# Top-32 attention and a quick-GELU MLP on one core: slots of two interleaved score tiles, packed array halves and MLP units of 128 tokens

## The chip, the cores and the metric

The kernel runs on one core of a Trainium2 chip. Its engines work side by side, each through its own list of instructions: TensorE (PE in the profile, with its loads of the stationary operand as PEld), VectorE (DVE), ScalarE (ACT), GpSimd (POOL), and SyncE (SP), which here issues DMAs. The metric is the device time of one execution in microseconds; lower is better. The kernel before takes 2505.77 us, the median of three runs from 2504.82 to 2506.19 us.

## The reference

```python
scores = scale * np.matmul(q, k.transpose(0, 1, 3, 2))        # q, k, v: (8, 8, 576, 64), scale 1/8
kth = np.partition(scores, -top_k, axis=-1)[..., -top_k:-top_k + 1]   # top_k = 32
scores = np.where(scores >= kth, scores, -1000000000.0)
attn = np.exp(scores - np.max(scores, axis=-1, keepdims=True))
attn = attn / (np.sum(attn, axis=-1, keepdims=True) + 1e-09)
x = np.matmul(attn, v).transpose(0, 2, 1, 3).reshape(4608, 512)
h = x @ w_in                                                   # (512, 2048)
return (h * (1.0 / (1.0 + np.exp(-1.702 * h))) @ w_out).astype(np.float32)   # (2048, 512)
```

All of it is in float32. The two weights come as float64, and the kernel rounds their bits to float32 itself.

## The kernel before

The 64 heads go in 32 pairs. `transpose_pair` turns q and k of a pair so that the first head's 64 dimensions lie on partitions 0 to 63 and the second's on 64 to 127. A head has 576 queries: four tiles of 128 rows, and a ninth tile of the pair that holds the last 64 rows of both. `scores` (from L167) multiplies a tile (`sc`, L181) into PSUM: 512 and 64 columns, contracted over the 64 partitions of its head. There the scores stay. VectorE finds the 32nd largest of each row in four rounds: the eight largest (MAX8, L185 and L196), then their removal (MATCH_VALUE_LOAD and MATCH_REPLACE8, L193), three times. Meanwhile GpSimd makes the negated maximum (`low`, L187), ScalarE the exponentials of all 576 scores (`e`, L189), and at the end VectorE multiplies these by the comparison with the 32nd largest (`pr`, L198).

`transpose_probs` (L208, L211) turns `pr` on TensorE, five transposes to a tile, and ScalarE copies them to SBUF as `pt`. `values` (L224) takes `pt` as the stationary operand and v, with a column of ones beside it for the denominators, as the moving one of 65 columns; VectorE takes reciprocals (L232, L234) and ScalarE divides (L236). `transpose_out` (L259, L262) turns the outputs of a pair once more into `xT`.

The MLP runs in twelve units of 384 tokens. `hidden` (L285) makes 128 hidden units of 384 tokens from four products; ScalarE takes tanh (L294) and VectorE the gate (L295). `project` (L304) multiplies with `wout` into 512 columns. The 32 pieces of weights, one to each of the first 32 tiles, are rounded by four VectorE instructions (L124, L127, L130, L131), one on ScalarE (L132) and four on GpSimd (L133 to L136).

The order of the program is a loop over tiles (from L342): each step issues the scores and the top-k of one tile, then what `at` put down for it from earlier tiles, then as many pieces of the MLP as a credit in columns allows. The framework's own scheduler then orders each engine's list. Every float32 product is two TensorE instructions in the trace, each with its load of the stationary operand; a transpose is one.

## Time and profile before

| | before |
|---|---|
| median of three runs | 2505.77 us (2504.82 to 2506.19) |
| span of the profiled execution | 2504.9 us |
| TensorE busy | 2276.3 us (91%) |
| VectorE busy | 1949.9 us (78%) |
| ScalarE busy | 686.9 us (27%) |
| GpSimd busy | 265.5 us (11%) |
| mean granted clock of TensorE | 0.881 of full speed |

The profiled execution has no time beside its span; the span stands 0.9 us under the median of the runs. Busy is the time in which an engine has at least one instruction in work; TensorE's instructions are pipelined, so lengths of single ones add up to more than that, and the start of the next instruction tells more than the end of one. The granted clock is TensorE's: 1.00 is 2.4 GHz and 0.50 is 1.2 GHz, its two levels. A rate is read from starts in the rows in order of time.

### The profile page before, as it was taken

The page shows a single profiled execution, that of the slowest core. Times are in us where ns is not written, and L with a number is a line of the kernel's source. Part 1 is how long each engine was busy: PE and PEld are TensorE (multiplying, and loading weights), DVE is VectorE, ACT ScalarE, POOL GpSimd, SP SyncE. Part 2 cuts the span into 40 slices and gives each one's busy share as a digit, 9 for nine tenths or more (in the row PEclk, how much of TensorE's full clock was granted, in tenths as well). Part 3 has the DMA queues.
Part 4 walks back from the last instruction along what each step waited for, and adds up shares of the span by engine and source line. Part 5 has one row for each costly group of instructions (what it writes and reads, how often), then busy time and mean ns, then how long its engine had stood idle before and what let it go on. Part 6 is the DMA issues. An engine that isn't in the chain of part 4 may idle for free.

```text
span 2504.9 us, 25884 instructions
## 1 busy us (share of the span) xinstructions
PE 2276.3 (91%) x9088; PEld 1399.2 (56%) x9088; DVE 1949.9 (78%) x3680; ACT 686.9 (27%) x1637; POOL 265.5 (11%) x490
## 2 busy tenths in 40 slices
PE   5556879998999999999999999999999999999999
PEld 3344556655655565665555565565555555665554
DVE  6999878887888888888888887888888887798200
ACT  2222223222222332232222332232322332232200
POOL 5777100000000000000000000000000000000000
PEclk9755559995789899999899999999899998999999
DMA  3222000000000000000000000000000000000000
GB/s 105 82 77 72 15 14 11 19 23 15 5 15 23 19 15 19 19 15 23 10 15 23 19 15 18 19 15 23 19 5 23 19 15 24 4 6 9 4 13 13
DMA packets 122818, 56.21 MB, mean 22 GB/s; under 512 B 116288, under 2 KB 116288, under 8 KB 122688
## 3 DMA queue, kind: packets, MB, share of 16 engines
q1 hardware_dynamic: 119808, 45.11, 7.1%
q0 software_dynamic: 2880, 9.44, 1.0%
q8 instruction: 73, 1.20, 0.2%
q14 instruction: 57, 0.47, 0.1%
HBM read 45.09 MB, written 9.44 MB: 22 GB/s over the span
## 4 chain that ended last, share of the span: by engine, by line
PE 72%; DVE 12%; issue 9%; POOL 4%; ACT 2%; SPq 0%; DMA 0%; POOLq 0%; ACTq 0%
PE ph L285 19%; PE po L304 17%; PE o L224 15%; PE sc L181 13%; PE tp L208 5%; DVE left L193 4%; DVE top L196 3%; ACT e L189 1%; PE tp L163 1%; DVE top L185 1%; PE tp L211 1%; POOL room L135 1%; POOL room L134 1%; POOL room L133 1%; DVE pr L198 1%
## 5 line engine op out<-in xcount | busy, mean ns | idle before, releaser
L196 DVE MAX8 top<-left 128x8 f32<-128x576 f32 x864 | 656.2, 759 | 22.3
L285 PE MATMUL ph<-xT,win 128*128 128x384 f32 x1536 | 563.5, 515 | 4.2 <-ACT xp L236 4.2
L304 PE MATMUL po<-wout,gT 128*128 128x512 f32 x1152 | 543.1, 614 | 2.1 <-ACT ob L313 2.1
L224 PE MATMUL o<-v_l,pt 128*128 128x65 f32 (+3 forms) x3200 | 499.4, 305 | 2.6 <-ACT pt L209 2.6
L224 PEld LDWEIGHTS o<-v_l,pt 128*128 128x128 f32 (+3 forms) x3200 | 440.1, 208 | 70.7 <-issue 11.5
L181 PE MATMUL sc<-k_t,q_t 64*128 64x512 f32 (+3 forms) x1280 | 450.4, 510 | 0.4 <-ACT k_t L164 0.4
L193 DVE MATCH_REPLACE8 left<-top,left 128x576 f32<-128x576 f32 x576 | 427.4, 742 | 0.0
L208 PE MATMUL tp<-ident,pr 128*128 128x128 f32 x1152 | 207.4, 310 | 209.4 <-DVE pr L198 205.1
L285 PEld LDWEIGHTS ph<-xT,win 128*128 128x128 f32 x1536 | 290.7, 198 | 189.1 <-issue 20.8
L189 ACT ACTIVATE e<-sc,low 128x576 f32<-128x576 f32 x288 | 213.2, 740 | 551.5 <-POOL low L187 551.4
L181 PEld LDWEIGHTS sc<-k_t,q_t 64*128 64x128 f32 (+1 forms) x1280 | 216.6, 204 | 238.7 <-issue 237.7
L304 PEld LDWEIGHTS po<-wout,gT 128*128 128x128 f32 x1152 | 210.4, 193 | 224.4 <-issue 207.8
L208 PEld LDWEIGHTS tp<-ident,pr 128*128 128x128 f32 x1152 | 158.3, 160 | 311.7 <-issue 289.5
L209 ACT COPY pt<-tp 128x512 f32<-128x512 f32 x288 | 168.6, 585 | 332.9 <-PE tp L208 332.5
L295 DVE SCALAR_TENSOR_TENSOR gT<-th,ph 128x384 f32<-128x384 f32 x192 | 105.8, 551 | 191.2 <-ACT th L294 190.5
L187 POOL TENSOR_SCALAR low<-top 128x1 f32<-128x1 f32 x288 | 64.6, 224 | 1699.1 <-DVE top L185 1665.9
L198 DVE SCALAR_TENSOR_TENSOR pr<-sc,top,e 128x576 f32<-128x576 f32 x288 | 230.4, 800 | 0.0
L185 DVE MAX8 top<-sc 128x8 f32<-128x576 f32 x288 | 215.4, 748 | 10.3 <-PE sc L181 10.1
L193 DVE MATCH_REPLACE8 left<-top,sc 128x576 f32<-128x576 f32 x288 | 215.4, 748 | 0.0
L294 ACT ACTIVATE th<-ph 128x384 f32<-128x384 f32 x192 | 94.3, 491 | 379.8 <-PE ph L285 379.8
L236 ACT ACTIVATE xp<-o,rden 128x64 f32<-128x64 f32 (+1 forms) x320 | 75.6, 313 | 230.3 <-DVE rden L234 230.3
L193 DVE MATCH_VALUE_LOAD left<-top,sc 128x8 f32 x288 | 26.5, 92 | 128.8 <-ACT e L189 125.2
(48 smaller groups left out, 865.5 us busy)
## 6 DMA issues: line engine op xcount, KB each, us to landing
out_dram<-ob POOLq DMA_DIRECT2D x36, 256.0 KB, 2.3
q_l<-in_q_dram SPq DMA_DIRECT2D x64, 128.0 KB, 2.4
k_l<-in_k_dram SPq DMA_DIRECT2D x64, 128.0 KB, 2.5
v_l<-in_v_dram SPq DMA_DIRECT2D x64, 128.0 KB, 2.4
room<-in_moe_w_in_dram SPq DMA_DIRECT2D x16, 512.0 KB, 3.8
room<-in_moe_w_out_dram SPq DMA_DIRECT2D x16, 512.0 KB, 3.4
q_l<-in_q_dram SPq DMA_DIRECT2D x32, 32.0 KB, 2.3
k_l<-in_k_dram SPq DMA_DIRECT2D x32, 32.0 KB, 2.4
```

Source lines behind the costliest of these rows:

```text
L181: nc.tensor.matmul(sc[rows, c], lhsT=d["qT"][on, cols], rhs=d["kT"][on, c])
L185: nc.vector.max(top[:], sc)
L189: nc.scalar.activation(e[:], sc, AF.Exp, bias=low[:])
L193: nc.vector.match_replace(nxt[:], top[:], left, LOWEST)
L196: nc.vector.max(top[:], left)
L198: nc.vector.scalar_tensor_tensor(out=pr[:], in0=sc, scalar=top[:, 7:8], in1=e[:], op0=ALU.is_ge, op1=ALU.mult)
L208: nc.tensor.transpose(full[:, c * P : (c + 1) * P], pr[:, c * P : (c + 1) * P], ident[:])
L209: nc.scalar.copy(out=pt[:, 0:NF, :].rearrange("p c r -> p (c r)"), in_=full[:, 0:FULL])
L224: nc.tensor.matmul(o[0:rows, g, :], lhsT=d["pt", s][0:keys, c, cols], rhs=d["v"][0:keys, c, j, :], start=(c == 0), stop=(c == NS - 1),)
L285: nc.tensor.matmul(ph[:, 0:UNIT], lhsT=win[:, c, f * P : (f + 1) * P], rhs=xts[m][:, c, u * UNIT : (u + 1) * UNIT], start=(c == 0), stop=( ...
L295: nc.vector.scalar_tensor_tensor(out=mlp["gT"][:, f, :], in0=th[:], scalar=1.0, in1=ph[:, 0:UNIT], op0=ALU.add, op1=ALU.mult)
L304: nc.tensor.matmul(po[:], lhsT=mlp["gT"][:, f, r * P : (r + 1) * P], rhs=wout[:, f, :], start=(f == 0), stop=(f == FC - 1),)
```

## The change

- A slot takes two score tiles: the same 128 queries of both heads of a pair, or the last 64 queries of two pairs. There are 18 slots to a batch, 144 in all. Their score products alternate between the heads, whose operands lie on opposite 64 partitions, and go to two PSUM tiles in pieces of 288 columns. ScalarE copies both to SBUF.
- VectorE's top-k alternates between the two tiles, instruction by instruction. Its last step no longer multiplies: it writes the negated score, and one less that for scores that are left out. Scores are 1/256 of their size, so that the exponential, taken afterwards with a scale of -256, is 0 for these. ScalarE sums the denominators in the same instruction, and GpSimd divides the probabilities.
- The last 64 columns of the two tiles lie side by side and are turned together (nine transposes for two tiles). For the value product v is now the stationary operand, 64 columns wide, and the turned probabilities move; the two heads write opposite halves of the output's partitions. The outputs come out as `xT`, so no transposes follow.
- The MLP's units are 128 tokens. One slot has a quarter of a unit: 16 hidden products of 128 columns, one tanh, one gate of 512 columns, four projections.
- In the first eleven slots three pieces of weights each are rounded, with temporaries in two buffers; one GpSimd step of before becomes ScalarE's absolute value, and the last is VectorE's.
- The order is written by hand: the framework's scheduler is off, and `slot(n)` fixes what each engine does. Outputs are stored from SyncE's queue.

```diff
-    UNIT = 384
+DOWN = 256.0
+    G = 4
+    FIRST = (TAIL, 0)
+    MAIN = (0, FULL + 2 * TAIL)
...
+    raws = pool("raws", 5)
+    temps = pool("temps", 2)
+    scp = pool("scp", 3)
+    prp = pool("prp", 2)
+    ps_s = pool("ps_s", 2, space=PSUM)
+    ps_t = pool("ps_t", 2, space=PSUM)
+    ps_h = pool("ps_h", 1, space=PSUM)
+    ps_p = pool("ps_p", 1, space=PSUM)
...
+        power = temps.tile([P, PIECE], F32, name="power")
+        part = temps.tile([P, PIECE], F32, name="part")
+        size = temps.tile([P, PIECE], F32, name="size")
+        nc.scalar.mul(out=part[:], in_=low, mul=2.0**-52)
+        nc.scalar.activation(size[:], high.bitcast(F32), AF.Abs)
...
+        def powers():
+            nc.vector.tensor_single_scalar(power[:].bitcast(U32), bits, 0xFF800000, op=ALU.bitwise_and)
+            nc.gpsimd.tensor_tensor(out=part[:], in0=part[:], in1=power[:], op=ALU.mult)
+            nc.gpsimd.tensor_tensor(out=part[:], in0=part[:], in1=dst, op=ALU.add)
+        def normal():
+            nc.vector.scalar_tensor_tensor(
+                out=dst, in0=size[:], scalar=LEAST_HIGH, in1=part[:], op0=ALU.is_ge, op1=ALU.mult
+            )
+        return [cut, sign, powers], normal
...
+    slots = []
+    for b in range(B):
+        slots += [(b, t, (hp, hp)) for t in range(NF) for hp in range(NP)]
+        slots += [(b, NF, (hp, hp + 1)) for hp in range(0, NP, 2)]
+    N = len(slots)
...
+    def scores(n):
+        b, t, hps = slots[n]
+        ps = [ps_s.tile([P, 2, 512], F32, name="s_ps") for _ in range(2)]
+        if t < NF:
+            parts = [(j, j, slice(0, P), slice(t * P, (t + 1) * P)) for j in range(2)]
+        else:
+            parts = [(i, j, slice(j * TAIL, (j + 1) * TAIL), slice(FULL, S)) for i in range(2) for j in range(2)]
+        for c in range(2):
+            for i, j, rows, cols in parts:
+                on = slice(j * D, (j + 1) * D)
+                nc.tensor.matmul(
+                    ps[i][rows, c, 0:HALF],
+                    lhsT=qT[b, hps[i]][on, cols],
+                    rhs=kT[b, hps[i]][on, FIRST[i] + c * HALF : FIRST[i] + (c + 1) * HALF],
+                )
+        sc = st[n]["sc"] = scp.tile([P, 2, S], F32, name="sc")
+        for i in range(2):
+            nc.scalar.copy(out=sc[:, i, :].rearrange("p (c k) -> p c k", c=2), in_=ps[i][:, :, 0:HALF])
+    def topk(n):
+        sc = st[n]["sc"]
+        top = st[n]["top"] = small.tile([P, 2, TOPK], F32, name="top")
+        left = lefts.tile([P, 2, S], F32, name="left")
+        def largest(r, i):
+            nc.vector.max(top[:, i, 8 * r : 8 * r + 8], (left if r else sc)[:, i, :])
+        def remove(r, i):
+            nc.vector.match_replace(
+                left[:, i, :], top[:, i, 8 * r : 8 * r + 8], (left if r else sc)[:, i, :], LOWEST
+            )
+        def leave_out(i):
+            nc.vector.scalar_tensor_tensor(
+                out=sc[:, i, :],
+                in0=sc[:, i, :],
+                scalar=top[:, i, TOPK - 1 : TOPK],
+                in1=sc[:, i, :],
+                op0=ALU.is_lt,
+                op1=ALU.subtract,
+            )
+        ops = []
+        for r in range(TOPK // 8):
+            ops += [lambda r=r, i=i: largest(r, i) for i in range(2)]
+            if r < TOPK // 8 - 1:
+                ops += [lambda r=r, i=i: remove(r, i) for i in range(2)]
+        return ops + [lambda i=i: leave_out(i) for i in range(2)]
+    def lowest(n):
+        low = st[n]["low"] = small.tile([P, 2], F32, name="low")
+        nc.gpsimd.tensor_scalar(low[:], st[n]["top"][:, :, 0], -DOWN, None, op0=ALU.mult)
+    def exponentials(n):
+        sc, low = st[n]["sc"], st[n]["low"]
+        pr = st[n]["pr"] = prp.tile([P, 2 * S], F32, name="pr")
+        den = st[n]["den"] = small.tile([P, 2], F32, name="den")
+        for i in range(2):
+            nc.scalar.activation(
+                pr[:, i * S : (i + 1) * S], sc[:, i, :], AF.Exp, bias=low[:, i : i + 1], scale=-DOWN,
+                accum_out=den[:, i : i + 1],
+            )
+    def divide(n):
+        den, pr = st[n]["den"], st[n]["pr"]
+        some = small.tile([P, 2], F32, name="some")
+        nc.vector.tensor_scalar_add(some[:], den[:], 1e-9)
+        rden = small.tile([P, 2], F32, name="rden")
+        nc.vector.reciprocal(rden[:], some[:])
+        for i in range(2):
+            on = pr[:, i * S : (i + 1) * S]
+            nc.gpsimd.tensor_scalar(on, on, rden[:, i : i + 1], None, op0=ALU.mult)
+    def turn(n):
+        pr = st[n]["pr"]
+        pt = st[n]["pt"] = ptp.tile([P, 2 * NF + 1, P], F32, name="pt")
+        for i in range(2):
+            tp = ps_t.tile([P, 512], F32, name="tp")
+            for c in range(NF):
+                nc.tensor.transpose(tp[:, c * P : (c + 1) * P], pr[:, MAIN[i] + c * P : MAIN[i] + (c + 1) * P], ident[:])
+            nc.scalar.copy(out=pt[:, i * NF : (i + 1) * NF, :].rearrange("p c r -> p (c r)"), in_=tp[:])
...
+    def values(n):
+        b, t, hps = slots[n]
+        pt = st[n]["pt"]
+        outs = []
+        if t < NF:
+            groups = [(0, [(j, slice(0, P), j) for j in range(2)])]
+        else:
+            groups = [(i, [(i, slice(j * TAIL, (j + 1) * TAIL), i) for j in range(2)]) for i in range(2)]
+        for i, heads in groups:
+            main, tail = vv[b, hps[i]]
+            o = ps_t.tile([P, 512], F32, name="o", tag="tp")
+            for c in range(NF + 1):
+                for j, (tile_, cols, half) in enumerate(heads):
+                    dst = o[j * D : (j + 1) * D, 0 : cols.stop - cols.start]
+                    if c < NF:
+                        lhsT, rhs = main[:, c, j, :], pt[:, tile_ * NF + c, cols]
+                    else:
+                        on = slice(half * TAIL, (half + 1) * TAIL)
+                        lhsT, rhs = tail[on, j, :], pt[on, 2 * NF, cols]
+                    nc.tensor.matmul(dst, lhsT=lhsT, rhs=rhs, start=(c == 0), stop=(c == NF))
+            outs.append((o, hps[i]))
...
+    def hidden():
+        if not ready:
+            return
+        xT, rows = ready[0]
+        g = hidden_at["g"]
+        ph = ps_h.tile([P, G, P], F32, name="ph")
+        for i in range(G):
+            f = g * G + i
+            for c in range(CC):
+                nc.tensor.matmul(
+                    ph[:, i, :],
+                    lhsT=win[:, c, f * P : (f + 1) * P],
+                    rhs=xT[:, c, :],
+                    start=(c == 0),
+                    stop=(c == CC - 1),
+                )
...
+            th = thp.tile([P, G, P], F32, name="th")
+            nc.scalar.activation(th[:], ph[:], AF.Tanh, scale=0.851)
+            to_gate.append((ph, g, rows, th))
+    def gate():
+        if to_gate:
+            ph, g, rows, th = to_gate.pop()
+            gT = gtp.tile([P, G, P], F32, name="gT")
+            nc.vector.scalar_tensor_tensor(
+                out=gT[:], in0=th[:], scalar=1.0, in1=ph[:], op0=ALU.add, op1=ALU.mult
+            )
+            to_project.append((gT, g, rows))
...
+    RATE = 3
+    by_slot = [list(range(i, min(i + RATE, NPIECE))) for i in range(0, NPIECE, RATE)]
+    for n, some in enumerate(by_slot):
+        for x in some:
+            at(n - 1, load_piece, x)
+    def slot(n):
+        todo = later.pop(n, [])
+        for fn, args in todo:
+            if fn is not prepare:
+                fn(*args)
+        if 0 <= n - 2 < N:
+            turn(n - 2)
+        if n >= NPIECE // RATE - NG + 1:
+            hidden()
+        if 0 <= n - 1 < N:
+            exponentials(n - 1)
+        if 0 <= n - 2 < N:
+            turn_tail(n - 2)
+        tanh()
+        rounding = [round_piece(x) for x in by_slot[n]] if 0 <= n < len(by_slot) else []
+        project()
+        for fn, args in todo:
+            if fn is prepare:
+                fn(*args)
+        if n + 1 < N:
+            scores(n + 1)
+        if 0 <= n - 2 < N:
+            values(n - 2)
+        chain = topk(n) if 0 <= n < N else [lambda: None] * 16
+        first = [op for ops, _ in rounding for op in ops]
+        last = [op for _, op in rounding]
+        for i, op in enumerate(chain):
+            op()
+            if i == 1 and 0 <= n < N:
+                lowest(n)
+            if i == 5 and 0 <= n - 1 < N:
+                divide(n - 1)
+            if i == 9:
+                gate()
+            if i and first:
+                first.pop(0)()
+            elif last and i > 11:
+                last.pop(0)()
+        for op in first + last:
+            op()
+    with tc.manual_schedule():
+        for n in range(-1, N + 2):
+            slot(n)
+        n = N + 2
+        while ready or to_project:
+            slot(n)
+            n += 1
```

`turn` makes eight transposes of `pr`, `turn_tail` the ninth; `load`, `load_v` and `prepare` are what `load_pair` and `transpose_pair` were, at fixed slots.

VectorE's list at a tile and a half in the middle of the kernel before, where `left` is the row with maxima removed, `top` the eight largest, and `gT` the gate:

```order
L185 MAX top<-sc 128x8
L198 SCALAR_TENSOR_TENSOR pr<-sc,top,e 128x576
L295 SCALAR_TENSOR_TENSOR gT<-th,ph 128x384
L193 MATCH_REPLACE left<-top,sc 128x576
L196 MAX top<-left 128x8
L193 MATCH_REPLACE left<-top,left 128x576
L232 TENSOR_SCALAR den<-o 128x4
L196 MAX top<-left 128x8
L234 RECIPROCAL rden<-den 128x4
L193 MATCH_REPLACE left<-top,left 128x576
L196 MAX top<-left 128x8
```

A whole slot on VectorE in the changed kernel:

```order
L239 MAX top<-sc 128x8 x2
L242 MATCH_REPLACE left<-top,sc 128x576 x2
L239 MAX top<-left 128x8 x2
L280 TENSOR_SCALAR some<-den 128x2
L282 RECIPROCAL rden<-some 128x2
L242 MATCH_REPLACE left<-top,left 128x576 x2
L239 MAX top<-left 128x8 x2
L382 SCALAR_TENSOR_TENSOR gT<-th,ph 128x512
L242 MATCH_REPLACE left<-top,left 128x576 x2
L239 MAX top<-left 128x8 x2
L247 SCALAR_TENSOR_TENSOR sc<-sc,top 128x576 x2
```

Before, each maximum and removal needs the one just ahead of it. Now two equal instructions follow each other, one for each tile, and what an instruction needs stands two places ahead.

TensorE's list for two tiles of before, where `sc` are scores, `tp` transposes, `o` values, `ph` hidden units and `po` projections:

```order
L208 MATMUL tp<-ident,pr 128x128 x4
L211 MATMUL tp<-ident,pr 64x128
L285 MATMUL ph<-xT,win 128x384 x2
L181 MATMUL sc<-k_t,q_t 128x512
L181 MATMUL sc<-k_t,q_t 128x64
L285 MATMUL ph<-xT,win 128x384 x6
L208 MATMUL tp<-ident,pr 128x128 x4
L211 MATMUL tp<-ident,pr 64x128
L181 MATMUL sc<-k_t,q_t 128x512
L181 MATMUL sc<-k_t,q_t 128x64
L285 MATMUL ph<-xT,win 128x384 x2
L224 MATMUL o<-v_l,pt 128x65 x15
```

A slot on TensorE in the changed kernel (`s_ps` are its scores, `v_l` and `v_t` the values' main part and last 64 rows):

```order
L293 MATMUL tp<-ident,pr 128x128 x8
L358 MATMUL ph<-xT,win 128x128 x16
L299 MATMUL tp<-ident,pr 128x128
L396 MATMUL po<-wout,gT 128x512 x4
L223 MATMUL s_ps<-k_t,q_t 128x288 x4
L323 MATMUL o<-pt,v_l 64x128 x8
L323 MATMUL o<-pt,v_t 64x128 x2
```

The hidden products have a third of the columns, and the value products write 64 partitions each; the scores are the next slot's, the turned probabilities and values those of two slots ago.

ScalarE's list in the weights' stage of before (`room` holds a piece's scaled low words) for two tiles:

```order
L189 ACTIVATE e<-sc,low 128x576
L209 COPY pt<-tp 128x512
L212 COPY pt<-tp 64x128
L132 ACTIVATE room<-room 128x512
L189 ACTIVATE e<-sc,low 128x576
L132 ACTIVATE room<-room 128x512
L209 COPY pt<-tp 128x512
L212 COPY pt<-tp 64x128
```

And one slot of the changed kernel in that stage (`part` are the scaled low words, `size` the absolute values):

```order
L294 COPY pt<-tp 128x512 x2
L272 ACTIVATE pr,den<-sc,low 128x576 x2
L300 COPY pt<-tp 128x128
L132 ACTIVATE part<-raw 128x512
L133 ACTIVATE size<-raw 128x512
L132 ACTIVATE part<-raw 128x512
L133 ACTIVATE size<-raw 128x512
L132 ACTIVATE part<-raw 128x512
L133 ACTIVATE size<-raw 128x512
L230 COPY sc<-s_ps 128x576 x2
L329 COPY xT<-o 128x128
```

The score copies for the next slot now stand behind the scaling of three pieces.

## Rows read from the trace of the kernel before

**Rows 1.** The page's head: span, TensorE's busy time, the chain that ended last.

```profile
span 2504.9 us, 25884 instructions
...
PE 2276.3 (91%) x9088; PEld 1399.2 (56%) x9088; DVE 1949.9 (78%) x3680; ACT 686.9 (27%) x1637; POOL 265.5 (11%) x490
...
PE 72%; DVE 12%; issue 9%; POOL 4%; ACT 2%; SPq 0%; DMA 0%; POOLq 0%; ACTq 0%
```

**Rows 2.** Line 185's instructions: duration min/median/max in ns, first and last start.

```profile
L185 DVE MAX8 top<-sc x288: 739/748/767, 10.1 to 2317.2; 128x8 f32<-128x576 f32 x144
```

**Rows 3.** TensorE in order of time: start, length in us, instructions [idle before <-releaser].

```profile
1197.69 3.70 PE L304 MATMUL po<-wout,gT 128*128 128x512 f32 x8
1201.23 0.60 PE L208 MATMUL tp<-ident,pr 128*128 128x128 f32 x4
...
1201.87 1.29 PE L181 MATMUL sc<-k_t,q_t 64*128 64x512 f32 x4
1203.09 1.47 PE L224 MATMUL o<-v_l,pt 128*128 128x65 f32 x10
1208.60 1.08 PE L208 MATMUL tp<-ident,pr 128*128 128x128 f32 x4 [4.04 <-DVE pr L198]
```

**Rows 4.** Stretches: us, busy PE, PEld, DVE, ACT, POOL, granted clock, DMA share, GB/s.

```profile
1208.70:1219.40 10.70, 10.70 (x37) 6.76 (x38) 9.32 (x19) 1.60 (x4) 0.29 (x2) 0.50 0.12 28
...
1062.60:1072.70 10.10, 10.10 (x27) 6.68 (x28) 4.59 (x11) 1.67 (x6) 0.15 (x1) 0.50 0.00 0
1072.80:1205.80 133.00, 131.07 (x571) 78.26 (x570) 113.33 (x218) 40.40 (x96) 5.59 (x22) 1.00 0.08 20
```

**Rows 5.** TensorE in order of time, ahead of the second of these stretches.

```profile
1058.77 4.42 PE L224 MATMUL o<-v_l,pt 128*128 128x65 f32 x30
```

**Rows 6.** VectorE in order of time, through parts of two tiles.

```profile
1604.72 0.76 DVE L196 MAX8 top<-left 128x8 f32<-128x576 f32 x1
1605.40 0.75 DVE L185 MAX8 top<-sc 128x8 f32<-128x576 f32 x1
1606.07 0.80 DVE L198 SCALAR_TENSOR_TENSOR pr<-sc,top,e 128x576 f32<-128x576 f32 x1
...
1607.33 0.75 DVE L193 MATCH_REPLACE8 left<-top,sc 128x576 f32<-128x576 f32 x1
1607.99 0.55 DVE L295 SCALAR_TENSOR_TENSOR gT<-th,ph 128x384 f32<-128x384 f32 x1
1608.45 0.75 DVE L196 MAX8 top<-left 128x8 f32<-128x576 f32 x1
1609.24 0.09 DVE L193 MATCH_VALUE_LOAD left<-top,left 128x8 f32 x1
1609.32 0.74 DVE L193 MATCH_REPLACE8 left<-top,left 128x576 f32<-128x576 f32 x1
```

**Rows 7.** TensorE's value products from one start, in two windows of different end.

```profile
1234.65 0.50 PE L224 MATMUL o<-v_l,pt 128*128 128x65 f32 x3
...
1234.65 0.72 PE L224 MATMUL o<-v_l,pt 128*128 128x65 f32 x5
```

**Rows 8.** TensorE in order of time: the ninth score tile of a pair.

```profile
1266.34 1.20 PE L181 MATMUL sc<-k_t,q_t 64*64 64x512 f32 x8
```

**Rows 9.** The page's groups: count, busy us, mean ns, idle time before.

```profile
L189 ACT ACTIVATE e<-sc,low 128x576 f32<-128x576 f32 x288 | 213.2, 740 | 551.5 <-POOL low L187 551.4
```

**Rows 10.** The same for the rounding of weights, shapes kept apart.

```profile
L133 POOL TENSOR_SCALAR room<-room 128x512 f32<-128x512 f32 x32 | 52.2, 1631 | 0.9 <-DVE room L131 0.9
...
L134 POOL TENSOR_TENSOR room<-room 128x512 f32<-128x512 f32 x32 | 40.6, 1268 | 54.7 <-DVE room L130 46.5 <-ACT room L132 6.4 <-ACT e L189 1.8
...
L127 DVE SCALAR_TENSOR_TENSOR wout<-room,wout 128x512 uint32<-128x512 uint32 x16 | 15.2, 953 | 0.0
...
L124 DVE TENSOR_SCALAR wout<-room 128x512 uint32<-128x512 uint32 x16 | 10.6, 664 | 0.0
```

**Rows 11.** ScalarE at the end of the span: the last output copy.

```profile
2499.47 0.60 ACT L313 ACTIVATE ob<-po 128x512 f32<-128x512 f32 x1 [13.19 <-PE po L304]
```

More of the change, by code (lines that the diff above doesn't have):

```diff
@@ new lines, with load @@
+    qT, kT, vv = {}, {}, {}
+    loaded = {}
+    def load(name, b, hp):
+        src = q if name == "q" else k
+        t = loaded[name, b, hp] = loads.tile([P, NF + 1, 2, D], F32, name=f"{name}_l")
+        for j in range(2):
+            nc.sync.dma_start(
+                t[:, 0:NF, j, :], src[b, 2 * hp + j, 0:FULL, :].rearrange("(t p) d -> p t d", p=P)
+            )
+        nc.sync.dma_start(
+            t[0:TAIL, NF, :, :], src[b, 2 * hp : 2 * hp + 2, FULL:S, :].rearrange("h p d -> p h d")
+        )
@@ L243, in head_values @@
-    def head_values(p, j):
-        values(p, [(j * NF + t, slice(0, P), j, t) for t in range(NF)], P)
-    def tail_values(p):
-        values(p, [(2 * NF, slice(j * TAIL, (j + 1) * TAIL), j, NF) for j in range(2)], TAIL)
-    xts = {}
-    def transpose_out(p):
-        b, hp = pairs[p]
-        xp = st.pop(p)["xp"]
-        if b // 2 not in xts:
-            xts[b // 2] = xtp.tile([P, CC, 2 * S], F32, name="xT")
-        dst = xts[b // 2][:, hp, b % 2 * S : (b % 2 + 1) * S]
+        tail = vals.tile([P, 2, D], F32, name="v_t")
@@ L312, in project @@
+    def project():
+        if not to_project:
+            return
+        gT, g, rows = to_project.pop(0)
+        if g == 0:
+            proj["po"] = ps_p.tile([P, C], F32, name="po")
+        po = proj["po"]
+        for i in range(G):
+            f = g * G + i
+            nc.tensor.matmul(
+                po[:], lhsT=gT[:, i, :], rhs=wout[:, f, :], start=(f == 0), stop=(f == FC - 1)
+            )
+        if g == NG - 1:
             ob = osp.tile([P, C], F32, name="ob")
             nc.scalar.mul(out=ob[:], in_=po[:], mul=0.5)
-            row = (m * PER + u) * UNIT + r * P
```

343 lines of the change are left out of this document (115 added, 228 removed).

## The prediction

> **What bounds the kernel now.** I read the page's head first: TensorE is busy for 91% of 2504.9 us, VectorE for 78%, and the chain that ended last runs 72% over TensorE, 12% over VectorE and 9% over issue [rows 1]. So TensorE sets the end, but not alone. The first maxima of the 288 score tiles spread from 10.1 to 2317.2 us [rows 2]: (2317.2 - 10.1) / 287 x 2 = 16.1 us for two tiles, the unit in which I count. Next the instructions in order of time on TensorE [rows 3]: a turned tile, its scores and its values follow one another without a gap, until the next tile's probabilities are late and TensorE stands 4.04 us behind VectorE. Last, the granted clock [rows 4]: after that stop TensorE ran 10.7 us at half clock (1.2 GHz), and the same turning of a tile took 1.08 us instead of 0.60. The clock fell another time without a stop, after 30 value instructions in a row [rows 5], and stayed at the full 2.4 GHz for 133 us of mixed work [rows 4]. Both engines are therefore near the bound, and each makes the other late.
>
> **VectorE, per slot of two tiles.** The count of its large instructions stays: eight maxima, six removals, two compares. What changes is their order. In a chain through one tile a removal's value load starts 0.79 us after its maximum of 0.75, so 0.04 behind its end; where neighbours do not need each other, a maximum is followed after 0.68 and 0.67 us, a removal after 0.66, each some 0.08 before its end [rows 6]. In the new order the instruction that is needed always stands two places back. So: 8 x 0.675 = 5.40; 6 x (0.08 value load + 0.66) = 4.44; two compares of 0.80 us, less the 0.08 that independent neighbours overlap, taken as 0.70 since both operands now lie in SBUF, 1.40; the gate, 0.46 us for 384 columns [rows 6] and so at most 0.61 for 512, 0.60; two small ones for the denominators, together 0.2. The sum is 12.0 us. The removal of a tile's first maximum, which ScalarE's exponential held up between 1606.07 and 1607.33 [rows 6], no longer waits for it: the exponential is taken a slot later.
>
> The Trainium skill, "VectorE: DVE Perf Modes", section "The DRAIN you can't avoid", says that the next instruction does not start until the pipeline is empty and that leaving out waits gains nothing. By that rule the slot would come to the dependent figure of the rival below; rows 6 disagree, since a maximum of 0.76 us was followed after 0.68.
>
> **TensorE, per slot, at full clock.** Turning: five transposes take 1201.87 - 1201.23 = 0.64 us [rows 3], so nine take 1.15. Hidden units: 32 instructions (each float32 product is two) with 128 columns and a new stationary operand each. That form is not in the trace; the nearest is the value product, which also loads 128 x 128 for each instruction: three take 0.50 and five 0.72, so one adds 0.11 [rows 7]. Its 65 columns might hide less than 128, but 512 columns take 3.54 / 8 = 0.44 [rows 3], so 128 need 0.11 too. If both run side by side, 32 x 0.11 = 3.52, which is also the floor; one after the other, 7.04. I take 3.52, since the transposes, which load 128 and stream 128, take 0.13. Projection: the eight instructions between 1197.69 and 1201.23, 3.54 [rows 3]. Scores: the ninth tile of a pair of heads already has its two parts in opposite quarters of the array, and its eight instructions take 1.20 us in all [rows 8]; an ordinary tile's four, with the same columns on one half, take 1.22 [rows 3]. A new slot streams the same columns through each half (4 x 288 = 2 x 576), so 1.20; without overlap, 2.44. Values: ten instructions now take 1.47 [rows 3]; a slot has 20, ten on each column half, so 1.47 with overlap and 2.94 without. No row shows two column halves with all 128 rows; I take overlap, as with the quarters. Queries and keys: eight calls of five transposes in 18 slots, 8 x 0.64 / 18 = 0.28. The sum is 11.2 us, below VectorE's 12.0. The turning back of the outputs is gone (its inputs come out transposed), which saves TensorE work only.
>
> So VectorE sets the slot, with 0.8 us to spare on TensorE. How much cover is there? TensorE's slot opens when GpSimd has divided, at 8.2 us of VectorE's slot before (below); 1.15 + 3.52 + 3.54 + 0.28 + 1.20 = 9.7 us later the next scores are there, and two copies of at most 0.74 us [rows 9] end at 19.4, where VectorE asks for them at 24.0: 4.6 us early. The gate, due 7.2 us into the slot, finds its tanh about 4 us old. The slots of the last 64 rows have scores and values twice and no preparation, 11.2 + 2.4 = 13.6 us; two such slots running use 3.2 us of that cover and cost nothing. Without it, 16 x 1.6 = 26 us.
>
> **The other engines.** ScalarE has some eleven instructions per slot, none longer than the exponential's 0.74 [rows 9] by much: under 8.2 us. The copies of scores to SBUF are its new work, and VectorE pays nothing for them, as they are made a slot ahead. GpSimd divides two tiles: 576 columns each by its 1.27 and 1.63 us for 512 [rows 10], 2.9 to 3.7 us, begun 4.4 us into a slot and done by 8.2, before the turning that needs it must start; VectorE's compares, the next with two SBUF operands, come at 10.6.
>
> **The first eleven slots** also round three pieces of weights each. Per piece VectorE has a cut (0.66), a sign (0.95), a power and a final product (bounded by the same two rows, as both forms lie between them) [rows 10], less 0.08 each: 2.8 us, 8.5 per slot, on 11.4 without a gate, 19.9. There is one new wait. Temporaries have two buffers and there are three pieces, so ScalarE's scaling of the third stands until VectorE has finished the first, and the score copies of the next slot are queued behind it. GpSimd's two products (2 x 1.27 us, rows 10) then follow before VectorE's last product: about 1.2 us of waiting, 21 us a slot. In slots 0 to 2 queries and keys are prepared behind the same wait, some 2.7 us more. 3 x 23.7 + 7 x 21 + 17 (two pieces) = 235, with four gates 237; from 200 (no collision with GpSimd) to 272 (3 us lost in each). TensorE has (1.15 + 1.20 + 1.47 + 0.28) x 2 = 8.2 us of work in such a slot before the MLP, even at half clock.
>
> **Start and end.** The first maximum came at 10.1 us [rows 2]. Now values are loaded ahead of the first queries, and scores are copied first: 14. At the end one unit of 128 tokens per slot is still due after the last top-k: two slots that turn and multiply the last probabilities, some 15 us, then five of hidden and projection at 3.52 + 3.54, one projection, and the 5.4 us from the last output copy's start at 2499.47 to the span's end [rows 11], with small waits: 67.
>
> **The sum.** 14 + 237 + 133 x 12.0 + 67 = 1914 us of span. The span before was 2504.9 against a median of 2505.77, so 1 us lies around it: 1915 us.
>
> **Rivals.**
> Column halves do not overlap, while row halves do: TensorE's slot is 11.2 + 1.47 = 12.6, TensorE is the bound, + 0.6 x 133: about 2000. For it: no row shows such a pair. 10%.
> Neither overlaps: 13.9 a slot, about 2165. Against it, rows 8. 6%.
> VectorE keeps its dependent spacing, 0.04 behind each end: 8 x 0.79 + 6 x (0.08 + 0.78) + 2 x 0.84 + 0.8 = 14.0 a slot in all 144: about 2200. Against it, rows 6. 5%.
> Loading and streaming of a 128-column hidden unit come one after the other: 14.7 a slot, about 2275. 8%.
> The other side: TensorE's clock falls. At half clock its slot is 22.4 us. Its short instructions (turning, scores, values) stand together in each slot, beside a short wait for the division, and rows 5 show a fall after a run of value products alone. If half clock holds in 43% of the 133 slots' time, the gain is gone: (2505 - 1915) / 133 = 4.4 us of 10.4; at half of it, about 2600. Against it: 133 us at full clock with the same mix [rows 4], and 7 of the 11.2 us of a slot are hidden and projection products without a break. 5%.
> The Trainium skill, "TensorE: Matmul & The Clock Gate", section "Why this matters for your kernels", warns for thin matmuls like these of 128 tokens that the clock oscillates unless products follow densely. No run here shows it for this form; by that rule the last rival would hold.
> Waits that I have not named, such as between GpSimd's division, the turning and the gate: 8%, 1960 to 2400.
>
> **Numbers.** The forecast has 58%, and by itself 1860 to 1975. The range 1850 to 2200 takes in the first two rivals, half of the third and of the unnamed waits, and leaves out slow hidden units and the clock. A measurement of this kernel can tell 0.2% from no change. Faster 0.94, within 0.2% 0.01, slower 0.05.
>
> **What would show it.** Right: VectorE over 90% busy from slot 11 on, maxima of one slot and the next 12 us apart, a granted clock near 1 there, hidden instructions 0.11 us apart, score and value instructions starting in pairs. Wrong: slots of 12.6 us or more with TensorE waited for; hidden instructions 0.2 apart; maxima starting 0.79 us after one another; half clock in most slots; a first stage far from 250 us.

## The result, and the profile after

The changed kernel takes 1917.39 us, the median of four runs from 1916.82 to 1919.22. The kernel before took 2505.98 us beside it; the ratio is 0.7652, with a 95% interval from 0.7641 to 0.7663. The forecast was 1915 us, with a range from 1850 to 2200.

The head of the page after: span, busy times, granted clock in 40 slices, the chain that ended last by engine, and two groups of the costliest.

```profile
span 1915.5 us, 31954 instructions
...
PE 1663.6 (87%) x11856; PEld 1181.9 (62%) x11856; DVE 1812.6 (95%) x3728; ACT 810.5 (42%) x1861; POOL 624.4 (33%) x502
...
PEclk9756799999999999999999999999999999999999
...
PE 44%; DVE 39%; POOL 10%; issue 4%; ACT 1%; SPq 0%; DMA 0%; POOLq 0%; DVEq 0%; ACTq 0%
...
L239 DVE MAX8 top<-left 128x8 f32<-128x576 f32 x864 | 612.0, 747 | 0.0
...
L358 PE MATMUL ph<-xT,win 128*128 128x128 f32 x4096 | 489.0, 279 | 0.0
```

Against [rows 1], VectorE has taken TensorE's place: it is busy for 95% of the span, against 78% before. The chain that ended last is walked back from the end, where TensorE works alone; it still names TensorE a little more often (44% against 39%), so the two engines run nearly level. Which of them sets the slot is read from the stretches. These are the first eleven slots, the full slots and the end: us, busy PE, PEld, DVE, ACT, POOL, granted clock, DMA share, GB/s.

```profile
15.00:260.00 245.00, 105.33 (x619) 76.68 (x620) 230.25 (x416) 91.55 (x195) 138.97 (x97) 0.75 0.29 83
260.00:1845.00 1585.00, 1486.66 (x10794) 1054.63 (x10792) 1570.19 (x3293) 703.47 (x1633) 480.16 (x396) 1.00 0.09 22
1845.00:1916.00 71.00, 65.10 (x422) 46.41 (x422) 10.71 (x20) 11.50 (x25) 4.32 (x3) 1.00 0.04 12
```

VectorE is busy for 1570 of the middle 1585 us (99%), TensorE for 94%. The clock is 1.00 there, where [rows 4] had stretches of 0.50. VectorE through one slot of after (start, length, instructions in a row):

```profile
1007.03 1.41 DVE L239 MAX8 top<-sc 128x8 f32<-128x576 f32 x2
1008.36 0.07 DVE L242 MATCH_VALUE_LOAD left<-top,sc 128x8 f32 x1
1008.42 0.74 DVE L242 MATCH_REPLACE8 left<-top,sc 128x576 f32<-128x576 f32 x1
1009.08 0.08 DVE L242 MATCH_VALUE_LOAD left<-top,sc 128x8 f32 x1
...
1014.24 0.67 DVE L382 SCALAR_TENSOR_TENSOR gT<-th,ph 128x512 f32<-128x512 f32 x1
1014.82 0.08 DVE L242 MATCH_VALUE_LOAD left<-top,left 128x8 f32 x1
...
1017.61 1.53 DVE L247 SCALAR_TENSOR_TENSOR sc<-sc,top 128x576 f32<-128x576 f32 x2
1019.05 1.41 DVE L239 MAX8 top<-sc 128x8 f32<-128x576 f32 x2
```

The slot is 1019.05 - 1007.03 = 12.02 us. Two maxima take 1008.36 - 1007.03 = 1.33 us of it, 0.67 each, not the 0.79 of the dependent pair in [rows 6]. TensorE beside it:

```profile
1005.02 3.74 PE L358 MATMUL ph<-xT,win 128*128 128x128 f32 x32
1008.60 0.27 PE L299 MATMUL tp<-ident,pr 128*128 128x128 f32 x1
1008.71 3.60 PE L396 MATMUL po<-wout,gT 128*128 128x512 f32 x8
1012.24 1.24 PE L223 MATMUL s_ps<-k_t,q_t 64*128 64x288 f32 x8
1013.41 1.09 PE L323 MATMUL o<-pt,v_l 128*64 128x128 f32 x16
1014.43 0.44 PE L323 MATMUL o<-pt,v_t 64*64 64x128 f32 x4
1014.80 1.15 PE L293 MATMUL tp<-ident,pr 128*128 128x128 f32 x8
1015.79 3.74 PE L358 MATMUL ph<-xT,win 128*128 128x128 f32 x32
```

From start to start, hidden units take 3.58 us (0.112 for an instruction), projection 3.53, scores 1.17, values 1.39, turning 1.10: 10.77 without the preparation of queries and keys. In this slot nothing like the 4.04 us of [rows 3] stands ahead of a turning. Over the middle 1585 us TensorE is idle for 98, and 91 of these are waits of a turning for GpSimd's division (101 times, the longest 3.6 us): that is TensorE waiting for a slot that VectorE sets.

### The profile page after: what moved, and what is told of

The parts are those of the page before. It is cut to its first block, busy times and chain, and to the rows that moved or that the text cites. A ratio compares the mean times of both kernels' runs of the same rounds, so it can differ in the third digit from the quotient of the medians.

```text
span 1915.5 us, 31954 instructions
## 1 busy us (share of the span) xinstructions
PE 1663.6 (87%) x11856; PEld 1181.9 (62%) x11856; DVE 1812.6 (95%) x3728; ACT 810.5 (42%) x1861; POOL 624.4 (33%) x502
## 4 chain that ended last, share of the span: by engine, by line
PE 44%; DVE 39%; POOL 10%; issue 4%; ACT 1%; SPq 0%; DMA 0%; POOLq 0%; DVEq 0%; ACTq 0%
DVE top L239 17%; PE ph L358 15%; PE po L396 15%; DVE left L242 13%; POOL pr L285 9%; PE o L323 5%; PE s_ps L223 4%; DVE sc L247 3%; PE tp L293 3%; DVE gT L382 2%; PE tp L196 1%; POOL part L147 1%; POOL part L148 1%; DVE power L146 1%; DVE rden L282 1%
## 5 line engine op out<-in xcount | busy, mean ns | idle before, releaser
L285 POOL TENSOR_SCALAR pr<-pr,rden 128x576 f32<-128x576 f32 x288 | 496.4, 1735 | 407.7 <-DVE rden L282 266.2
L358 PE MATMUL ph<-xT,win 128*128 128x128 f32 x4096 | 489.0, 279 | 0.0
L358 PEld LDWEIGHTS ph<-xT,win 128*128 128x128 f32 x4096 | 478.7, 196 | 0.5 <-issue 0.5
L272 ACT ACTIVATE pr<-sc,low 128x576 f32<-128x576 f32 x288 | 221.0, 768 | 243.7 <-DVE sc L247 243.3
L230 ACT COPY sc<-s_ps 128x576 f32<-128x576 f32 x288 | 169.8, 642 | 285.5 <-PE s_ps L223 285.5
L247 DVE SCALAR_TENSOR_TENSOR sc<-sc,top 128x576 f32<-128x576 f32 x288 | 231.2, 841 | 0.0
L223 PE MATMUL s_ps<-k_t,q_t 64*128 64x288 f32 (+1 forms) x1280 | 202.6, 436 | 1.6 <-ACT k_t L197 1.6
L223 PEld LDWEIGHTS s_ps<-k_t,q_t 64*128 64x128 f32 (+1 forms) x1280 | 114.6, 183 | 93.5 <-issue 71.1
L323 PEld LDWEIGHTS o<-pt,v_l 128*64 128x64 f32 x2560 | 128.2, 138 | 59.8 <-issue 42.2
L323 PE MATMUL o<-pt,v_l 128*64 128x128 f32 (+1 forms) x2560 | 163.7, 271 | 0.0
```

The costliest lines, as they stand in the source:

```text
L223: nc.tensor.matmul(ps[i][rows, c, 0:HALF], lhsT=qT[b, hps[i]][on, cols], rhs=kT[b, hps[i]][on, FIRST[i] + c * HALF : FIRST[i] + (c + 1) * ...
L230: nc.scalar.copy(out=sc[:, i, :].rearrange("p (c k) -> p c k", c=2), in_=ps[i][:, :, 0:HALF])
L247: nc.vector.scalar_tensor_tensor(out=sc[:, i, :], in0=sc[:, i, :], scalar=top[:, i, TOPK - 1 : TOPK], in1=sc[:, i, :], op0=ALU.is_lt, op1= ...
L272: nc.scalar.activation(pr[:, i * S : (i + 1) * S], sc[:, i, :], AF.Exp, bias=low[:, i : i + 1], scale=-DOWN, accum_out=den[:, i : i + 1],)
L285: nc.gpsimd.tensor_scalar(on, on, rden[:, i : i + 1], None, op0=ALU.mult)
L323: nc.tensor.matmul(dst, lhsT=lhsT, rhs=rhs, start=(c == 0), stop=(c == NF))
```

## The experiments

The theory: VectorE sets the slot, because its instructions now stand so that none needs its neighbour, and TensorE fits beneath because array halves overlap. Each of the first three kernels takes one part of that away; the others follow the cost that is left.

**Order on VectorE.** One tile's chain after the other's, same instructions:

```diff
         chain = topk(n) if 0 <= n < N else [lambda: None] * 16
+        chain = chain[0::2] + chain[1::2]
...
-            if i == 1 and 0 <= n < N:
+            if i == 8 and 0 <= n < N:
```

> One tile's whole top-k chain, then the other's; all else as in the changed kernel (only the negated maxima are taken seven instructions later). If the gain on VectorE comes from the order alone, each value load and maximum again starts 0.04 us behind the end of what it needs instead of 0.08 before its neighbour's end: a slot of 13.6 to 14.0 us instead of 12.03, so 2150 to 2190 us. TensorE would then idle some 3 us a slot; if its clock falls for that, longer still. The rival, that the scores' place in SBUF gives the spacing whatever the order: 1917 us.

Measured 2125.39 us, ratio to before 0.8482 (0.8469 to 0.8495). The middle slot is 13.59 us: 1.56 x 133 = 207 of the 208 us lost. VectorE in that kernel:

```profile
1006.03 0.09 DVE L242 MATCH_VALUE_LOAD left<-top,left 128x8 f32 x1
1006.11 0.74 DVE L242 MATCH_REPLACE8 left<-top,left 128x576 f32<-128x576 f32 x1
1006.89 0.76 DVE L239 MAX8 top<-left 128x8 f32<-128x576 f32 x1
1007.68 0.09 DVE L242 MATCH_VALUE_LOAD left<-top,left 128x8 f32 x1
```

A dependent instruction starts 0.03 to 0.04 us behind the end of the one it needs (1006.89 + 0.76 to 1007.68), where in the changed kernel an instruction starts 0.08 ahead of its neighbour's end. So 208 us of the gain hang on the order alone, and the rival, that the scores' place in SBUF gives the spacing, is out. The slot is the low end of what was expected, and yet the time is 25 us below its range: the first eleven slots did not grow (236.3 us beside 236.1), where the rounding of weights stands between the dependent instructions.

**Column halves.** Both heads' values into partitions 0 to 63, one after the other; ScalarE copies them apart:

```diff
-            o = ps_t.tile([P, 512], F32, name="o", tag="tp")
+            o = [ps_t.tile([P, 512], F32, name="o", tag="tp") for _ in range(2)]
...
-                    dst = o[j * D : (j + 1) * D, 0 : cols.stop - cols.start]
+                    dst = o[j][0:D, 0 : cols.stop - cols.start]
...
-                nc.scalar.copy(out=xts[b, t][:, hp, :], in_=o[:, 0:P])
...
+                    nc.scalar.copy(out=xts[b, t][j * D : (j + 1) * D, hp, :], in_=o[j][0:D, 0:P])
...
```

> Both heads' value products write the lower 64 partitions, so they share one column half; two copies per slot, not one, bring them to their places. The theory from the trace after: 20 products of 128 columns at 0.107 us one after the other, 2.2 us instead of 1.4, so TensorE's slot is 11.6 us, still under VectorE's 12.03: 1917 us, within 0.3%. The rival with the prediction's price (1.47 us more, TensorE the bound at 12.3 to 12.6): 1950 to 2000 us.

Measured 1983.48 us, 0.7916 (0.7904 to 0.7928): the expectation missed, and the time lies in the rival's range. TensorE:

```profile
1006.94 1.96 PE L323 MATMUL o<-pt,v_l 128*64 128x128 f32 x16
1008.84 0.44 PE L323 MATMUL o<-pt,v_t 64*64 64x128 f32 x4
```

Sixteen products take 1.90 us, not 1.02, so halves do overlap in the changed kernel. The median slot stays at 12.05, but the mean is 12.48: three to five slots around the end of each batch take 13 to 14.3 us. Two waits over the whole run (us in all, times, longest), that of TensorE's turning for the copies of the outputs and VectorE's for the denominators, in this kernel:

```profile
PE tp L293 <- ACT xT L329: 129.1, 119, 14.8
...
DVE some L280 <- ACT pr L272: 48.4, 44, 2.8
```

And in the changed kernel:

```profile
PE tp L293 <- ACT xT L329: 53.7, 7, 8.5
...
DVE some L280 <- ACT pr L272: 1.0, 1, 1.0
```

The denominators wait for exponentials, and these stand in ScalarE's queue behind the copies of turned probabilities, which wait for TensorE. TensorE's mean slot is 11.15 us (next run), and 0.88 more makes 12.03, VectorE's own slot: no cover is left for the uneven ones. The loss showed in the slots with more TensorE work, not in all; of the 66 us, 7 stand behind the last compare. But the edit does a second thing. The two tiles `o` take both buffers in turn with `tp`, so that the next turning waits until ScalarE has copied them: in the full slots 109 times, at most 0.4 us each and 47 us in all, where the changed kernel has no such wait. TensorE's slot thus grows by the halves' 0.88 and by up to 0.4 of the buffers'. That halves overlap is shown; that their overlap alone is worth 66 us is not, and no run separates the two.

**TensorE's own slot.** The fourth round of the top-k is left out:

```diff
-                scalar=top[:, i, TOPK - 1 : TOPK],
+                scalar=top[:, i, 23:24],
...
-        for r in range(TOPK // 8):
+        for r in range(3):
...
-            if r < TOPK // 8 - 1:
+            if r < 2:
...
```

> Leaves out the fourth round of the top-k, so that 24 scores are kept and not 32: two maxima and two removals less, 2 x 0.67 + 2 x 0.73 = 2.8 us of VectorE per slot. If TensorE stands right behind VectorE, the slot falls from 12.03 to TensorE's 10.8 and no further: 1917 - 133 x 1.2 - 11 x 2.8 = about 1725 us. If VectorE alone set the slot: 9.2 us and about 1515 us. If a round of waits between the engines (division, turning, gate) holds it at 12: no more than the first stage's 30 us, about 1885 us.

Measured 1797.68 us, 0.7173 (0.7162 to 0.7183). The middle of the run, columns as above:

```profile
260.00:1700.00 1440.00, 1432.16 (x10550) 1029.35 (x10548) 1194.01 (x2450) 678.91 (x1601) 470.00 (x387) 1.00 0.09 23
```

Now TensorE is the bound (1432 of 1440 us) and VectorE is not (1194). Slots are 10.8 us, with some of 11.2 to 13.1 at the end of each batch; the mean is 11.15. The expectation missed by 70 us: some 40 because it took 10.8 for all slots, and 23 because the first eleven slots gave 8 us and not the 31 it took off. With the 18 slots of a batch averaged, TensorE stands only 0.9 us below VectorE.

**The first eleven slots.** A third buffer for each temporary of the rounding (and one less for the raw words, for space):

```diff
-    raws = pool("raws", 5)
-    temps = pool("temps", 2)
+    raws = pool("raws", 4)
+    temps = pool("temps", 3)
```

> Three buffers for the rounding's temporaries, paid for with four instead of five for the raw weights. If ScalarE's wait for VectorE's first final product costs what the trace shows (1.2 us before the last product in each of ten slots, some 1 us before the next slot's scores in the first three): 12 to 15 us less, 1902 to 1905 us. The rival, that this time is lost elsewhere in the same slots, for instance to raw weights that come later: 1917 us.

Measured 1896.52 us, 0.7567 (0.7554 to 0.758): 21 us off the changed kernel, more than expected. The reason is in the changed kernel's slots, all engines in order of time:

```profile
52.13 0.66 ACT L132 ACTIVATE part<-raw 128x512 f32<-128x512 uint32 x1 [11.53 <-DVE win L151]
...
52.87 1.62 POOL L147 TENSOR_TENSOR part<-part,power 128x512 f32<-128x512 f32 x1 [2.35 <-ACT part L132]
...
53.28 1.82 DVE L247 SCALAR_TENSOR_TENSOR sc<-sc,top 128x576 f32<-128x576 f32 x1
...
56.26 0.69 DVE L151 SCALAR_TENSOR_TENSOR win<-size,part 128x512 f32<-128x512 f32 x1 [1.16 <-POOL part L148]
...
58.69 1.42 DVE L239 MAX8 top<-sc 128x8 f32<-128x576 f32 x2 [1.01 <-ACT sc L230]
```

ScalarE's third scaling waits for a buffer, GpSimd's product comes late, and three prices follow. VectorE waits 1.16 us for the last product, as was forecast (10.9 us in ten slots). In the first three slots it waits 1.0 us for score copies queued behind the scaling. And a compare that starts while GpSimd's product of 1.62 us runs takes 1.82 us instead of 0.81, and ends 0.61 us behind that product. This happens once in each of ten slots, at 1.81 to 1.82 us; no other compare of that kernel takes over 0.82. With three buffers no compare starts beside a product, all take 0.79 to 0.82, and the eleven slots fall from 236 to 214 us.

**The gate to GpSimd, ahead of the division.** VectorE's slot is the bound, and 0.58 us of it is the gate. GpSimd makes it as tanh x h + h, from a copy that ScalarE takes out of PSUM:

```diff
+            hs = hsp.tile([P, G, P], F32, name="hs")
+            nc.scalar.copy(out=hs[:], in_=ph[:])
...
-            nc.vector.scalar_tensor_tensor(
-                out=gT[:], in0=th[:], scalar=1.0, in1=ph[:], op0=ALU.add, op1=ALU.mult
-            )
+            nc.gpsimd.tensor_tensor(out=gT[:], in0=th[:], in1=ph[:], op=ALU.mult)
+            nc.gpsimd.tensor_tensor(out=gT[:], in0=gT[:], in1=ph[:], op=ALU.add)
...
-            if i == 9:
+            if i == 3:
```

> The gate moves from VectorE to GpSimd: ScalarE copies the hidden units to SBUF beside its tanh, and GpSimd makes th * h + h in two instructions, placed before its division. VectorE loses 0.59 us a slot; TensorE's 10.8 stays below the 11.44 that remain. If VectorE alone sets the slot: 133 x 0.59 = 78 us less, 1839 us. The rival: GpSimd's 2.6 us more delay the division, so that turning is late, or collide with VectorE's compares: little or no gain, 1880 to 1930 us.

Measured 1931.99 us, 0.7707 (0.7691 to 0.7722): slower than the changed kernel. The slots are as long as there (12.02 us on average); 10 us are lost behind the last compare, 75.3 against 65.6. The same with three buffers (and one buffer fewer for outputs, for space):

> The gate on GpSimd and three buffers for the rounding's temporaries (four raw buffers, one output buffer). If both effects are what they should be and add: 1824 to 1827 us. If the gate's move gains nothing, 1902 to 1905 us.

Measured 1913.28 us, 0.7633 (0.762 to 0.7646), 17 us above the run with the buffers alone. The trace of the first of the two, all engines in order of time:

```profile
1012.55 3.67 POOL L286 TENSOR_SCALAR pr<-pr,rden 128x576 f32<-128x576 f32 x2
...
1016.27 0.66 PE L294 MATMUL tp<-ident,pr 128*128 128x128 f32 x4 [1.10 <-POOL pr L286]
...
1016.77 3.74 PE L359 MATMUL ph<-xT,win 128*128 128x128 f32 x32
...
1020.81 0.60 ACT L376 ACTIVATE th<-ph 128x512 f32<-128x512 f32 x1
...
1021.30 0.59 ACT L378 COPY hs<-ph 128x512 f32<-128x512 f32 x1
...
1021.97 1.27 POOL L385 TENSOR_TENSOR gT<-th,hs 128x512 f32<-128x512 f32 x1 [5.57 <-ACT hs L378]
...
1023.33 1.27 POOL L386 TENSOR_TENSOR gT<-gT,hs 128x512 f32<-128x512 f32 x1
...
1024.58 1.72 POOL L286 TENSOR_SCALAR pr<-pr,rden 128x576 f32<-128x576 f32 x1
```

Division, turning, hidden units, tanh, copy, gate, and behind the gate the next division: every step waits for the one before, and from 1012.55 to the next division at 1024.58 it is 12.03 us. VectorE had become faster, but a ring over four engines set the slot. (Around 500 us the same ring took 11.8 us; the division there took 3.42 and not 3.67.)

**The ring cut.** Four kernels follow: the gate behind the division (at `i == 9` again, and with n < N on GpSimd; after the last slot VectorE gates); the gate of the slot before, issued ahead of the slot's small maximum; that with three buffers; and that with a sixth buffer for turned queries and keys. From the second on, gates and outputs have one buffer fewer and the copies of hidden units two; the last two pay for their buffers with raw ones. Of each only the lines that matter are shown.

```diff
             if i == 9:
-                gate()
+                gate(n < N)
```

> The trace of the last two runs showed why the gate on GpSimd gave nothing: GpSimd's two products (2.6 us) stood ahead of the division (3.67), waited for the copy of the hidden units, those for the hidden products (3.57), those for the turning (0.5), and that for the division of the slot before: a ring of 12.03 us. Here the products stand behind the division, so that the ring is cut (after the last slot the gate is VectorE's again). If the ring was all: ordinary slots fall to VectorE's 11.43, three slots per batch where the last rows and the preparation of queries and keys meet stay at 12.5 to 13.1: 250.7 + 132 x 11.45 + 27 + 78 = 1867. Rival: the products now run from 8.4 to 11.0 us of VectorE's slot, and its first compare, due at 10.0 with two SBUF operands, is held until they end, as it was by GpSimd's product among the weights: slots of about 12.4, 1960 to 1990.

Measured 1915.51 us, 0.7642 (0.763 to 0.7653).

```diff
         project()
+        if n < N:
+            gate(True)
...
-            if i == 9:
-                gate()
+            if i == 9 and n >= N:
+                gate(False)
```

> The gate of a slot's unit is taken by GpSimd at the start of the next slot, from data that is one slot old, so that it neither waits (no ring) nor runs beside the compares: ordinary slots 11.43, 250.7 + 132 x 11.45 + 27 + 80 = 1869. If something else than the ring and the compares holds the slots at 12.03, as TensorE with small waits, it is again 1920 to 1930.

Measured 1921.8 us, 0.7666 (0.7654 to 0.7679).

```diff
-    raws = pool("raws", 5)
-    temps = pool("temps", 2)
+    raws = pool("raws", 4)
+    temps = pool("temps", 3)
```

> The run before with three buffers of temporaries for the rounding of the weights, which gave 21 us by themselves: 1848. If the gate gains nothing: 1900.

Measured 1903.9 us, 0.7596 (0.7585 to 0.7608).

```diff
-    qkt = pool("qkt", 5)
+    qkt = pool("qkt", 6)
...
-    READY = ((-6, -5), (-2, -1), (-1, 0), (0, 1))
+    READY = ((-10, -9), (-6, -5), (-1, 0), (0, 1))
```

> The run before, with a sixth buffer for turned queries and keys, so that the second pair of heads is prepared four slots earlier, away from the slots of the last rows. If the three slots of 12.5 to 13.1 per batch are TensorE's, made so by the preparation that falls on them, two preparations of 0.64 us less there save 1 to 2 us in each of seven batches: 1835 to 1840. Rival: the double scores and values alone make them so: as the run before, 1848.

Measured 1903.36 us, 0.7594 (0.7583 to 0.7605). None of the four gave what the gate should give. All have slots of 12.0 us, and none of the slots at a batch's end is over 12.4; the second and third come near the figures set down for no gain (1920 to 1930, and 1900). The trace of the first of the four:

```profile
1004.76 1.28 POOL L388 TENSOR_TENSOR gT<-th,hs 128x512 f32<-128x512 f32 x1
...
1006.11 1.27 POOL L389 TENSOR_TENSOR gT<-gT,hs 128x512 f32<-128x512 f32 x1
...
1006.63 2.10 DVE L248 SCALAR_TENSOR_TENSOR sc<-sc,top 128x576 f32<-128x576 f32 x2
```

The ring is gone, but the second product now holds the first compare: 2.10 us for the two instead of 1.53, and the 0.57 lost is just what the gate had given. The rival named this collision and priced it at 1.0. In the second kernel the gate was written for the start of the next slot, but GpSimd does not wait for a slot: its list ran on behind the division, and the same collision came back.

**The gate where no compare is.** With three buffers, and the unit of the slot before, issued behind the small maximum, which GpSimd gets only after VectorE's first maxima of the slot:

```diff
                 lowest(n)
+                gate(True)
```

> In the four runs before, the trace shows that GpSimd ran the gate at once behind the division, since its data was there, and its second product held VectorE's first compare: the two compares took 2.06 to 2.10 us, not 1.53, and so the slot 12.0, not 11.43. Here the gate of the slot before stands behind the small scaled maximum, which GpSimd gets 1.7 us into VectorE's slot: products from 1.7 to 4.3 us, the division from 4.7, nothing beside the compares at 10.0. If the compares were all: ordinary slots 11.43, and with the first stage and end of the run with three buffers (234 and 87 us), 234 + 132 x 11.45 + 87 = 1833; with TensorE's three long slots in each batch up to 1860. Rival: something else (TensorE, the removals beside GpSimd's products) keeps 12.0: 1900.

Measured 1840.44 us (1840.1 to 1840.92), 0.7342 (0.733 to 0.7355). All engines in order of time:

```profile
1001.53 1.41 DVE L240 MAX8 top<-sc 128x8 f32<-128x576 f32 x2
...
1003.03 0.22 POOL L266 TENSOR_SCALAR low<-top 128x2 f32<-128x2 f32 x1 [4.81 <-DVE top L240]
...
1003.22 1.28 POOL L390 TENSOR_TENSOR gT<-th,hs 128x512 f32<-128x512 f32 x1
...
1004.57 1.27 POOL L391 TENSOR_TENSOR gT<-gT,hs 128x512 f32<-128x512 f32 x1
...
1006.30 3.43 POOL L286 TENSOR_SCALAR pr<-pr,rden 128x576 f32<-128x576 f32 x2 [0.46 <-DVE rden L283]
...
1011.59 1.53 DVE L248 SCALAR_TENSOR_TENSOR sc<-sc,top 128x576 f32<-128x576 f32 x2
...
1013.04 0.75 DVE L240 MAX8 top<-sc 128x8 f32<-128x576 f32 x1
```

The compares are back at 1.53, and the slot is 11.52 us (11.43 was expected). This version beats both kernels: 77 us below the changed kernel, of which 21 are the buffers' and 56 the gate's (67 in the 133 full slots, less 10 given back: 2 in the first eleven slots and 8 behind the last compare). In its middle 1500 us VectorE is busy for 1485 and TensorE for 1457, so little is left beneath.

With the second pair prepared earlier, as above:

```diff
-    READY = ((-6, -5), (-2, -1), (-1, 0), (0, 1))
+    READY = ((-10, -9), (-6, -5), (-1, 0), (0, 1))
```

> The run beside it, with the second pair of heads prepared four slots earlier. At 12.0 us a slot this made no difference (1903.4 beside 1903.9), since no slot at the end of a batch was long. At 11.43 they may be: then 5 to 12 us less than the run beside it; if TensorE's cover holds at 11.43 too, the same.

Measured 1840.27 us, 0.7341 (0.733 to 0.7352): the same, at 12.0 us and at 11.5. Preparing queries and keys elsewhere buys nothing while the cover holds.

Of the whole gain of 589 us, 208 are shown for the order on VectorE, and up to 66 for the column halves and their buffers. The rest came with parts that no run takes away singly, such as the outputs that need no turning back, the scores in SBUF and the order by hand.

## Why the prediction was right, point by point

- Start: 14 forecast, 13.2 measured.
- First eleven slots: 237 forecast, 236.1 measured. The parts erred both ways: the first three sum to 67.8 (forecast 71), the next seven to 151 (147), the last is 17.2 (17). The step was right that temporaries make VectorE wait, 1.16 us against 1.2. It left out that a compare is held as well, 1.0 us in each of ten slots. On the other side, the 2.7 us that it put on slots 0 to 2 were 1.0, in late score copies, and a slot without any of these waits takes 19.6 us, not 19.9, as the run with three buffers shows. That these errors nearly cancel is luck; the bound of 3 us per slot for collisions covered the first.
- VectorE's slot: 12.0 forecast, 12.03 measured. The first experiment shows that the order gives it, and the kernel with the gate where no compare is that the slot follows VectorE's work, down to 11.52. The section of the Trainium skill that the prediction found at odds with [rows 6], "The DRAIN you can't avoid" in "VectorE: DVE Perf Modes", was read too narrowly: it also says "A next op that is not held starts earlier". The trace agrees with that sentence, with independent maxima of 0.75 us 0.67 apart. Inside the slot, small errors cancel: a removal takes 0.72 with its load (forecast 0.74) and a maximum 0.665 (0.675), but the denominators cost 0.34 (0.2).
- TensorE's slot: 11.2 forecast; the three-round kernel measures 11.15 on average. The 0.11 us per hidden instruction, read from the value products in [rows 7], was 0.112, so loading and streaming do lie side by side. Row halves overlap as [rows 8] said (1.17), and so do column halves, for which no row stood (1.39 for a slot's values, against 1.90 + 0.37 = 2.27 on one half). The score instructions and the value instructions start in pairs, 6 to 7 ns apart, as the prediction asked.
- Cover: it held in the changed kernel, where no slot after the first eleven is over 12.4 us. In the slot shown the score copies end at 1014.74, 4.3 us before VectorE asks for them at 1019.05 (forecast 4.6). The slots of the last rows were over-priced: their two value tiles take 1.76 us in all, not 2.9. That without cover such slots cost was right in kind. Its price of 26 us is not tested: the run with one column half lost 66, but it lengthens every slot, by the halves and by the wait for buffers.
- The clock: 0.75 in the first stretch and 1.00 from 260 us on. The rival of half clock did not come. In the first experiment, where TensorE idles longer (241 us of 1783 in the full slots, against 98 of 1585), the clock over the full slots was 0.96. The Trainium skill, "TensorE: Matmul & The Clock Gate", section "Why this matters for your kernels", warns that thin matmuls let the clock oscillate unless they follow densely. These 128-token products do follow densely, 0.112 us apart, so by that rule the rival need not have held, though the prediction said that it would. The trace agrees: there is no half clock in the full slots but for 257 to 260 us and 400 to 407 us. Around the start of each of these TensorE waited twice for the division (1.79 and 1.04 us; 3.57 and 0.93 us), the second time behind a slot for which no unit was ready.
- End: 67 forecast, 65.6 measured from the end of the last compares at 1849.9.

The sum of the measured terms, 13.2 + 236.1 + 1600.5 + 65.6 = 1915.4, is the span but for rounding. Each of the four terms of the forecast erred by less than 5 us, and the errors partly cancelled. The mechanism is the one that was forecast: VectorE sets the slot at its independent spacing, and TensorE stays just beneath.

## What to carry to other kernels

When one engine's list sets the time, look for pairs of neighbours that need each other, and put independent work between them; that alone was worth 208 us here. When work moves to an idle engine, follow the ring through every queue that it joins, and look at what its operands do to the engine it was to relieve: the same gate on the same engine gave nothing in two places and 56 us in a third. A list does not wait for a slot; what holds an instruction back is the one ahead of it, or the data.

## What was not expected of the hardware

- VectorE's compare, whose two operands lie in SBUF, is held by a GpSimd product of two tensors that is already running: 1.82 us against 0.81 among the weights, 2.10 against 1.53 for two in the full slots. Where one operand lies in PSUM it was not: eleven compares of the kernel before started beside such products and took 0.79 to 0.80, and three gates of the changed kernel 0.66.
- An instruction can be held without two operands in SBUF. In the first eleven slots eight of ten cuts of the weights (one operand, 0.41 us alone) that started beside a product took 0.75 to 1.13, and nine additions to the denominators (128x2, 0.15 alone) 0.55 to 1.25; all ended 0.03 to 0.28 us behind the product.
- GpSimd's division by a scalar for each partition holds the compare far less: in the first kernel with the gate on GpSimd, two compares beside it took 1.65 (1.53 alone). Maxima and removals beside GpSimd's products kept their 0.67 and 0.72.
- ScalarE's exponential with a row sum leaves a second record, ACTIVATION_READ_ACCUMULATOR, of 0.19 us each time; it lies off the bound here.
